# Masked scores computed in two 64-key halves on two column groups of TensorE, with a new order from entry 480 on

## The chip, the cores and the metric

The kernel runs on one core of one Trainium2 chip. The metric is device time of one execution in microseconds (us). Each core has TensorE (PE, with its weight loads shown apart as PEld), VectorE (DVE), ScalarE (ACT), GpSimd (POOL) and SyncE (SP, which here issues most of the DMAs). Measured differences under about 0.5% count as none.

## The reference, cut to what matters

Two layers follow each other. The first is a linear recurrence over the sequence with a complex decay, for 4 batches, 8 heads, 768 positions and 48 dimensions; the second is a feed-forward layer with the activation h * tanh(softplus(h)).

```python
mag = np.sqrt(a_re * a_re + a_im * a_im)
scale = np.minimum(mag, 0.999) / (mag + 1e-06)
for t in range(S):
    S_re, S_im = (ar * S_re - ai * S_im + kv, ar * S_im + ai * S_re)   # kv = k[t] outer v[t]
    y[:, :, t] = np.einsum('bhd,bhde->bhe', q[:, :, t], S_re)
h = x @ w_in                      # x: 3072 tokens x 384, w_in: 384 x 2048
sp = np.where(h > 20.0, h, np.log1p(np.exp(np.minimum(h, 20.0))))
out = (h * np.tanh(sp)) @ w_out   # w_out: 2048 x 384
```

## The kernel before, in words

The work is cut into 12 units of 256 positions, three for each batch. A unit is two chunks of 128 positions, called u3a and u3b for unit 3.

For each unit, ACT and DVE first turn the decay into running magnitudes and phases and multiply q and k by their growth, sine and cosine (lines 449 to 546). DMAs on SP relay the result into a tile `T` per chunk, with 96 rows (48 cosine, 48 sine) and for each of the 8 heads 128 columns of q and 128 of k.

The attention of a chunk then runs on TensorE, in groups of four heads (g = 0 and 1):

- `kn` (line 609) transposes k into PSUM, and a copy brings it to SBUF.
- `am` (line 623) computes the scores, 128 keys by 128 queries for each head, into a PSUM tile `pa`: one matmul a head in the source. In the trace every fp32 matmul is two loads and two matmuls, so a group of four heads is eight matmuls.
- `am_out` (line 630, DVE) multiplies `pa` by the causal mask into the SBUF tile `am`. A query sees keys up to its own position, so a quarter of each score matrix (keys 64 to 127, queries 0 to 63) is all zero.
- `y` (line 641) adds `am` times V and the old state `S` times q in `ypsum`. Even heads write PSUM partitions 0 to 47 and odd heads 64 to 111, so a pair of heads uses the two column halves of the array.
- `pd` (line 656) computes the new state. Each head is two matmuls, of 64 and of 33 output rows, again on the two column halves. `S add` (lines 665, 667) follows on DVE.

The feed-forward part takes each unit's y as x. For each of 8 pairs of columns, `mm1` (line 751) fills a PSUM tile `ph`, then come exp, cap, square, ln and inv on ACT and DVE, `gate`, `gh` and `gl`, and `mm2` (line 788) adds into `po`. Here the matmul runs on fp32r, with each operand split in two halves (xH, xL, wh, wl, gh, gl).

Nothing schedules this at run time. All operations are recorded in a list and issued in the order of the table `ORDER` (lines 54 to 152), whose letters can pick the engine. Each engine then works its own queue strictly in that order and waits on semaphores. So PE's order decides which matmuls stand next to each other, and how much other PE work lies between a score group and the `ypsum` matmuls that read its mask product.

Of the kernel before, what the change touches and what calls it, by code (L numbers as in the profile page):

```python
# [45 lines left out]
HELD = 2  # L46
XRUNS = ((0, 0, 0, 32), (0, 1, 32, 16), (64, 1, 64, 16), (0, 2, 80, 32))
# [18 lines left out]
306 397 744 400 307 246V 398 446 299 401 257 248 579 322 396 399 308 402 249 403 448 405 580 313 748 404 250 406 323  # L66
# [3 lines left out]
342 602 598 338 331 425 344 604 427 268 269 601 339 463 749 747 345 609 270 346 462 607 751 261V 605 475 347 933 271V  # L70
444 599 340 752 348 608 606 754 474 756 932 349 757 341 437 458 419 350 464 456V 476 439 351 416 465 759 466 610 441
352 612 487 353 613 611V 354 443 750 614 355 600 477 467 753G 445 486 745 468 746 478 616 758 479 615 469 621 617 488
618 755 470 622 447 619 623 449 480 626 489 624 471 499 760 490 498 940 481 491 451 511 500 625 492 510 764 620 501
628 493 502 482A 494 522 761 503 512 472 454 513 523 763 453 504 627 473 937 505 630 762 629 455 524 631 514 483 535
515 525 765 526 766 534 516 495 767A 517 484 527 768 632 485 528 774 636 506 536 459 496 633 771 769 634 518 507 497
772 635 537 529 508 519 530A 509 773 775A 770 546 639 641 640 460 777 547 637 538 520 548 531 521 784 539 532 938 549
787 642 533 540 638 785 941G 550 541 778 643 551 457 786 939 644 779 542A 790 655 552 543 780 645 942 783 544 788 461
944 545 789 553 782 945 656 943 781 554 1123 668 555 953 646 791 657 954 793 946 556 955 792 794V 647 956 557 648 658
667 957 558 649 559 795 560 1124 650 659 561 1128V 797 947 796 669 679 798 651A 948 660 802 670 776 949 671 800 935
661 799 934 803 1129 804 958 936 806 1131 662 680 950 1130 691 681 672 807V 692 673 805 682 952 674 808 810 809 652  # L80
951 801V 812 683 811 653 693 813 663A 1133 684 814 965A 963 675A 815 685 961 817 816V 964A 960 819 664 654 959 686 823
694 825 665 962 967 824 1135 822 703 695 676 968 704 974 973 716 971 705 696 706 666 975 1144 1132 697 978 828 677 698
707 977 1136 966 1145 1305 715 970 830 687 976 728 717 972 708 718 727 688 969 709 1134 980 826 678 719 979 699 720
831 1304 689 710 721 1146 829 1137 690 700 729 818 1125 827 701 1138 1147 1126 711A 702 722 1139 832 820 1148 821 833
712 730 981 1312V 834 713 1140 723A 982 845 724 731 1141 983 985 984 732 714 733 1142 734 725 1309 1149 844 1143 735
835 856 736 836 1155G 986 1150 726 1154 1151V 1153 737 1152 987 1157 846 857 738 988 837 1158 838 992 739 994 741 993
740 839 1127 997 989 742 995 858 1156 847 1310 998V 990 996 848 1313G 999 991V 1163 1001 1000 840 1162 849 1003 1161
1311 841 1160 869 850 1002 1494 1314 842 851 1316 868 1004 1317 1325 1005 859 1006 1315 860 1008 1326 1164 861 1010
862 880 852A 1007V 1167 870 881 1493 871 1169 1011 872 863 843 1165 873 853 1013 882 892 874 1166 883 1318 875 1014
854 884 1327 1170 1319 893 1159 1320 864A 1016 1328 855 894 865 1015 885 1321 1168 905 886 895 1017 904 1009 896 1018  # L90
887 897 866 876 1307 906 1019V 877 898 1306 867 1501 1020 899 1498 878 907 888 908 1021V 1171 1022 1499 1173 900 917
1322 909 1172 916 910 1174V 879 918 919 1024 1329 920 1500 1502 1175 1324 1177 1176 1506 889 1023 921 911 1323 890
1012 922 1504 1335G 912A 891 1178 1025 1336G 1036 1026 1503 1180 1332V 1334 1179 1182 1330 901 1184 913 1035 923 1183
924A 902 1185 1331 1186G 903 914 925 1333 1685 1338 915 1027 1505 926 1028 1345 1339 927 1341 1514 1047 1037 1346 928V
1507 1038 1343 1515 1048 1039 1348 1029 1181V 1351 1187 1040 929 930 1030 1189 1308 1508 1340 1509 1060 1516 1049 1188
1344 1041 1190 931 1191 1342 1050 1337 1517 1192 1042 1059 1193 1031 1518 1051 1194 1032 1071 1052 1347 1510 1043A
1350 1033 1053 1349 1061 1072 1196 1062 1054 1063 1684 1034 1197 1064 1195 1073 1352 1065 1495 1354 1074 1083 1044
1055A 1496 1075 1056 1045 1689 1066 1692V 1076 1084 1202V 1511 1077 1096 1200 1690 1095 1198V 1085 1078 1067A 1199
1046 1201 1097 1519 1108 1079A 1086 1098 1087 1203 1057 1512 1068 1099 1058 1100 1069 1353 1080 1101 1513 1070 1088
1526G 1107 1355 1089 1356 1691 1090 1524 1358 1091A 1521 1081 1102 1204 1357 1109 1092 1205 1103 1082 1110 1359 1111  # L100
1217 1104 1206 1112 1363 1113 1360 1364 1207 1361 1694 1365 1693 1696 1367 1093 1368 1114 1362 1520 1115 1216 1525A
1366 1528 1094 1218 1208 1105 1116 1529 1209 1522V 1106 1219 1523 1117 1228 1697 1535 1118 1865 1369 1371 1533 1370
1220 1534 1373 1210 1372 1531 1119 1229 1121 1211 1122 1374 1241 1120 1230 1705 1497 1221 1231 1537 1240 1695 1232
1536 1233 1706 1375 1532 1234 1538 1376 1222 1530 1698 1223 1378 1866 1212A 1235 1539 1380 1699 1377V 1253 1242 1381
1386 1243 1540 1252 1213 1244 1383 1224A 1264 1541 1245 1225 1384 1246 1700 1214 1254 1701 1870 1265 1379 1236 1527
1255 1686 1215 1247 1256 1385 1871 1226 1237 1687 1266 1276 1257 1267 1707 1391V 1872 1248 1542 1702 1258 1544 1277
1392 1227 1708 1238 1259 1387V 1278 1389V 1239 1249 1268 1279 1269 1388 1288 1390 1270 1250 1873 1271 1704 1875 1874G
1289 1280 1382 1393 1281 1260A 1394 1545 1290 1261 1703 1251 1291 1272A 1876 1262 1282 1292 1716 1283 1263 1715A 1293
1273 1543 1284 1406 1878 1709 1710 1879 1546 1712V 1294 1548 1395 1295 1711 1274 1547 1881 1275 1549 1285 1877 1405
1714 1713 1553 1407 1555 1296 1286 1297 1718 1287 1298 1554 1556 1408 1396 1299 1409 1886 1397 1418 1398 1300V 1725  # L110
1399 1417 1410 1880 1558 1302V 1550 1727 1400 1719 1559V 1551 1401A 1688 1557 1419 1887 1560 1882 1730 1562 1561 1723
1552 1564 1722 1411 1563 1301 1430 1565 1720 1717 1303 1883 1566 1721 1726 1567 2055 1569 2054 1568V 1420 1571 1402
1421 1429 1575 1412 1422 1572 1731 1403 1431 1724 1423 1432 1576 1404 1433 1424 1729 1434 1413 1441 1577 1425A 1728
# [95 lines left out]
def tile_kernel(ctx, tc, q, k, v, are, aim, are_t, aim_t, w_in, w_out, out):  # L209
# [866 lines left out]
```

## Time and profile before

| | |
|---|---|
| three runs | 586.17, 586.56, 588.39 us (median 586.56) |
| profiled execution, first to last instruction | 585.6 us |
| PE busy / PEld busy | 574.0 us (98%) / 540.2 us (92%) |
| DVE busy / ACT busy / POOL busy | 470.4 us (80%) / 474.2 us (81%) / 24.1 us (4%) |
| mean granted TensorE clock | 0.997 |
| DMA | 67.10 MB, mean 115 GB/s |

The profiled execution is listed by its span alone. The runs' median lies 1.0 us above that span. A matmul's duration in the trace holds its way through the array, so neighbours overlap: the rate of a stream is read from the distance between starts, not from the duration of one.

### The profile page before, as it was taken

What the parts mean: (1) busy time and instruction counts of PE and PEld (TensorE: products, weight loads), DVE (VectorE), ACT (ScalarE), POOL (GpSimd) and SP (SyncE); (2) the same over time, 40 slices, a digit from 0 to 9 for tenths busy, and PEclk for the clock granted to TensorE, in tenths of its full rate; (3) what the DMA queues carried; (4) which work ended last, traced back from release to release, by engine and by line L of the source; (5) the groups of instructions that cost most, each with busy time, mean ns of one, the idle gap of its engine ahead of it and who ended that gap; (6) DMA issues with size and microseconds to landing.
All of it is one profiled execution on the core that took longest, in us unless ns stands there. A gap on an engine that the chain in (4) does not pass through costs nothing.

```text
span 585.6 us, 12607 instructions
## 1 busy us (share of the span) xinstructions
PE 574.0 (98%) x4974; PEld 540.2 (92%) x4974; DVE 470.4 (80%) x830; ACT 474.2 (81%) x762; POOL 24.1 (4%) x57
## 2 busy tenths in 40 slices
PE   8999999999999999999999999999999999999996
PEld 4679887899999999999999999999999999999995
DVE  6999999999999889886779978778777865465453
ACT  7899999899997999689988869876974966555572
POOL 2010000101000100000001001001000000000000
PEclk9999999999999999999999999999999999999998
DMA  8788865403637252280081082272064042001000
GB/s 288 256 258 268 282 223 152 140 4 93 176 85 188 73 152 77 65 235 2 26 215 59 2 241 58 55 216 56 10 177 113 1 125 84 32 8 28 29 1 31
DMA packets 57170, 67.10 MB, mean 115 GB/s; under 512 B 4832, under 2 KB 50144, under 8 KB 57104
## 3 DMA queue, kind: packets, MB, share of 16 engines
q1 hardware_dynamic: 56320, 65.37, 37.8%
q8 instruction: 41, 0.67, 0.5%
q10 hardware_dynamic: 720, 0.66, 0.4%
q14 instruction: 25, 0.20, 0.1%
q0 software_dynamic: 64, 0.20, 0.1%
HBM read 37.75 MB, written 4.72 MB: 73 GB/s over the span
## 4 chain that ended last, share of the span: by engine, by line
PE 61%; ACT 18%; DVE 12%; issue 4%; DMA 2%; SPq 1%; POOL 0%; DVEq 0%; ACTq 0%; POOLq 0%
PE ph L751 25%; PE po L788 23%; ACT e L173 6%; ACT X L173 5%; PE ypsum L641 4%; PE pa L623 4%; ACT L171 4%; PE pd L656 2%; PE pkn L609 2%; DVE g L764 1%; DVE am L630 1%; DVE gl L776 1%; DVE X L546 1%; ACT I L173 1%; DVE e L820 1%
## 5 line engine op out<-in xcount | busy, mean ns | idle before, releaser
L173 ACT ACTIVATE e<-e 128x512 f32<-128x512 f32 x192 | 118.2, 627 | 32.7 <-DVE e L820 31.4
L751 PE MATMUL ph<-xH,wh 128*128 128x256 f32 x462 | 133.3, 288 | 0.8 <-DVE g L764 0.7
L751 PE MATMUL ph<-xH,wl 128*128 128x256 f32 x462 | 129.8, 281 | 0.0
L751 PE MATMUL ph<-xL,wh 128*128 128x256 f32 x462 | 129.7, 281 | 0.0
L788 PE MATMUL po<-wh,gh 128*128 128x384 f32 x308 | 105.1, 341 | 0.0
L788 PE MATMUL po<-wh,gl 128*128 128x384 f32 x308 | 103.8, 337 | 0.0
L788 PE MATMUL po<-wl,gh 128*128 128x384 f32 x308 | 103.5, 336 | 0.0
L751 PEld LDWEIGHTS ph<-xH,wh 128*128 128x128 f32 x462 | 87.0, 188 | 3.3 <-DVE g L764 1.7
L751 PEld LDWEIGHTS ph<-xL,wh 128*128 128x128 f32 x462 | 87.0, 188 | 0.3
L751 PEld LDWEIGHTS ph<-xH,wl 128*128 128x128 f32 x462 | 87.0, 188 | 0.0
L764 DVE SCALAR_TENSOR_TENSOR g<-e,ph 128x512 f32<-128x512 f32 x96 | 65.3, 681 | 27.0 <-ACT e L173 25.2
L173 ACT ACTIVATE e<-ph 128x512 f32<-128x512 f32 x96 | 56.5, 590 | 33.3 <-PE ph L751 28.9
L776 DVE TENSOR_TENSOR gl<-g,gh 128x512 fp32r<-128x512 f32 x88 | 60.0, 684 | 15.1 <-ACT gh L770 9.4
L173 ACT ACTIVATE e<-e,fifth 128x512 f32<-128x512 f32 x96 | 68.8, 719 | 1.3
L820 DVE TENSOR_SCALAR e<-e 128x512 f32<-128x512 f32 x96 | 40.2, 421 | 25.3 <-ACT e L173 25.0
L788 PEld LDWEIGHTS po<-wh,gl 128*128 128x128 f32 x308 | 57.9, 188 | 0.7 <-DVE gl L776 0.5
L788 PEld LDWEIGHTS po<-wh,gh 128*128 128x128 f32 x308 | 58.0, 188 | 0.3 <-issue 0.2
L788 PEld LDWEIGHTS po<-wl,gh 128*128 128x128 f32 x308 | 57.9, 188 | 0.0
L171 ACT ACT_TABLE_LOAD x44 | 56.5, 1283 | 0.7
L623 PE MATMUL pa<-T 96*128 96x128 f32 x384 | 49.4, 277 | 0.8 <-DVE am L630 0.8
L623 PEld LDWEIGHTS pa<-T 96*128 96x128 f32 x384 | 46.1, 191 | 2.0 <-DVE am L630 1.0
L770 ACT CAST gh<-g 128x512 fp32r<-128x512 f32 x43 | 26.3, 611 | 12.2 <-DVE g L764 11.8
(137 smaller groups left out, 1049.3 us busy)
## 6 DMA issues: line engine op xcount, KB each, us to landing
T<-QK SPq DMA_DIRECT2D x70, 129.0 KB, 3.1
T<-X SPq DMA_DIRECT2D x69, 129.0 KB, 3.2
words<-w_in SPq DMA_DIRECT2D x8, 768.0 KB, 5.8
words<-w_out SPq DMA_DIRECT2D x8, 768.0 KB, 5.0
QK<-k SPq DMA_DIRECT2D x12, 384.0 KB, 4.4
QK<-q SPq DMA_DIRECT2D x12, 384.0 KB, 4.3
V<-v SPq DMA_DIRECT2D x12, 384.0 KB, 4.4
R<-a_re SPq DMA_DIRECT2D x12, 384.0 KB, 4.0
```

Source lines behind the costliest of these rows:

```text
L171: self.nc.scalar.preload_act_table_set(need)
L173: return self.nc.scalar.activation(out, in_, func, **kw)
L609: e.transpose(d["pkn", g][:, i, :], T()[:, 4 * g + i, 1, :C], ident)
L623: e.matmul(d["pa", g][:, i, :], T()[:, 4 * g + i, 1, :C], T()[:, 4 * g + i, 0, :C], start=True, stop=True)
L641: e.matmul(ypsum[64 * par:64 * par + D, i, :], lhs, rhs, start=m == 0, stop=first or m == 1)
L656: e.matmul(d["pd", g][r, i, :], d["kn"][:, h, r], st["V"][:, c, h * D:(h + 1) * D], start=not held, stop=not held or i == 3)
L751: e.matmul(ph[k][:, slot(k, j, a), :], win(x, j, kt, a), st[y][:, kt, cols(k)], start=n == 0, stop=n + 1 == len(todo))
L764: e.scalar_tensor_tensor(g_[k], e_[k], 2.5, ph[k], ALU.subtract, ALU.mult)
L770: (e.copy if e is nc.scalar else e.tensor_copy)(gs[k][0], g_[k])
L776: e.tensor_tensor(gs[k][1], g_[k], gs[k][0].bitcast(F32), ALU.subtract)
L788: e.matmul(po[t], x[:, slot(k, j, a), 0 if halved else t * P:C if halved else (t + 1) * P], wout(y, j, a), start=j == 0 and a == 0 and n == 0,
L820: op("V", f"{n} cap", lambda e, k=k: e.tensor_scalar_min(e_[k], e_[k], math.exp(20.0)))
```

## The change

From unit 3 on (`HALF = 3`) a group of four heads is computed by halves of 64 keys. The first half (keys 0 to 63) meets all 128 queries, the second (keys 64 to 127) only queries 64 to 127; the quarter that the mask makes zero isn't computed. The even head of a pair writes keys 0 to 63 to PSUM partitions 0 to 63, the odd head to partitions 64 to 127, and for the second half the other way round, so that at any time one head of the pair is on either column half. In the odd heads the key rows are thus swapped, and a second copy of V for the odd heads with its rows rolled by 64 (`vs`, prepared outside the kernel and loaded by a DMA for each unit) takes V's place in `y`.

The mask product is written by three DVE instructions in place of one, into two tiles that are kept for the whole kernel and were set to zero once. The mask constant has a second copy for the swapped rows. `ORDER` keeps its first 480 entries; the rest is another order. One line of the table's difference stands for all.

```diff
+HALF = 3
-306 397 744 400 307 246V 398 446 299 401 257 248 579 322 396 399 308 402 249 403 448 405 580 313 748 404 250 406 323
+306 397 744 400 307 246V 398 446 299 401 257 248 579 322 396 399 308 402 249 403 448 405 580 313 749 404 250 406 323
...
-    cmask = const.tile([P, P], BF16, name="cmask")
-    nc.gpsimd.memset(cmask, 1.0)
-    nc.gpsimd.affine_select(
-        out=cmask, in_=cmask, compare_op=ALU.is_ge, fill=0.0, base=0,
-        pattern=[[1, P]], channel_multiplier=-1,
-    )
+    cmasks = const.tile([P, 2, P], BF16, name="cmask")
+    cmask = cmasks[:, 0]
+    nc.gpsimd.memset(cmasks, 1.0)
+    for r0, par, base in ((0, 0, 0), (0, 1, -64), (64, 1, 0)):
...
+    swapped = Tiles({"Vs": (wts, "w14", 1, [P, 2, NCH, DM // 2])})
+    masked = Tiles({g: (at, "am", 2, [P, 4, C]) for g in range(2)})
...
+        if u >= HALF:
+            st.homes["Vs"] = lambda: swapped["Vs"][:, u % 2]
+            op("S", f"Vs{u} load", lambda e: e.dma_start(st["Vs"], vs[u]))
...
-                    for i in range(4):
-                        e.matmul(d["pa", g][:, i, :], T()[:, 4 * g + i, 1, :C], T()[:, 4 * g + i, 0, :C],
-                                 start=True, stop=True)
+                    if u < HALF:
+                        for i in range(4):
+                            e.matmul(d["pa", g][:, i, :], T()[:, 4 * g + i, 1, :C], T()[:, 4 * g + i, 0, :C],
+                                     start=True, stop=True)
+                        return
+                    for i0 in (0, 2):
+                        for k0 in (0, C // 2):
+                            for i in (i0, i0 + 1):
+                                r0 = (k0 + C // 2 * (i % 2)) % C
+                                e.matmul(d["pa", g][r0:r0 + C // 2, i, k0:], T()[:, 4 * g + i, 1, k0:k0 + C // 2],
+                                         T()[:, 4 * g + i, 0, k0:C], start=True, stop=True)
...
+                    d["am", g] = masked[g]
+                    x, y = (t.rearrange("p (i two) t -> p i two t", two=2) for t in (d["am", g], d["pa", g]))
+                    m = cmasks.unsqueeze(1).broadcast_to([P, 2, 2, C])
+                    for r, two, t in ((slice(0, P), slice(0, 2), slice(C // 2, C)),
+                                      (slice(0, P // 2), 0, slice(0, C // 2)), (slice(P // 2, P), 1, slice(0, C // 2))):
+                        e.tensor_tensor(x[r, :, two, t], y[r, :, two, t], m[r, :, two, t], ALU.mult)
...
-                                lhs = st["V"][:, c, h * D:(h + 1) * D] if new else old["S"][:, h, :]
+                                if u >= HALF and par:
+                                    lhs = st["Vs"][:, c, i * D:(i + 1) * D]
+                                else:
+                                    lhs = st["V"][:, c, h * D:(h + 1) * D]
+                                lhs = lhs if new else old["S"][:, h, :]
...
+        if u == HALF:
+            for g in range(2):
+                op("GV", f"masked{g} zero", lambda e, g=g: e.memset(masked[g], 0.0))
```

PE's queue at the scores of u3a, in the kernel before: `pa` is the score tile, `ph` and `po` belong to the feed-forward part.

```order
L751 MATMUL ph<-xH,wl 128x256
L623 MATMUL pa<-T 128x128 x8
L751 MATMUL ph<-xH,wh 128x256
L751 MATMUL ph<-xL,wh 128x256
L751 MATMUL ph<-xH,wl 128x256
```

The same scores of u3a in the changed kernel (64x128 is a first half, 64x64 a second):

```order
L824 MATMUL po<-whl,gh 128x384
L644 MATMUL pa<-T 64x128 x2
L644 MATMUL pa<-T 64x64 x2
L644 MATMUL pa<-T 64x128 x2
L644 MATMUL pa<-T 64x64 x2
L644 MATMUL pa<-T 64x128 x2
L644 MATMUL pa<-T 64x64 x2
L644 MATMUL pa<-T 64x128 x2
L644 MATMUL pa<-T 64x64 x2
L824 MATMUL po<-whl,gh 128x384
```

Eight source matmuls become sixteen narrower ones, still between matmuls that use the full array. The scores of u7b in the kernel before stand between a transpose and `ph`, with no matmul of the column halves beside them:

```order
L641 MATMUL ypsum<-am,V 48x128 x2
L609 MATMUL pkn<-identity,T 128x96 x4
L623 MATMUL pa<-T 128x128 x8
L751 MATMUL ph<-xH,wh 128x256
L751 MATMUL ph<-xL,wh 128x256
```

In the changed kernel u7b's scores (one group of four heads here, the other group behind the last of these rows) stand between `ypsum` matmuls of u7a (`kept` is the kept mask product, `Vs` the rolled copy of V):

```order
L674 MATMUL ypsum<-kept,V 48x128
L674 MATMUL ypsum<-kept,Vs 48x128
L644 MATMUL pa<-T 64x128 x2
L644 MATMUL pa<-T 64x64 x2
L644 MATMUL pa<-T 64x128 x2
L644 MATMUL pa<-T 64x64 x2
L674 MATMUL ypsum<-T,S 48x128 x2
L674 MATMUL ypsum<-kept,V 48x128
L674 MATMUL ypsum<-kept,Vs 48x128
```

Here the scores moved next to work that also uses the column halves. Over the whole of PE's queue, blocks of matmuls on the column halves, each entered from and left to full-array matmuls, are 32 before and 40 now.

DVE's queue at the mask product of u3a, before, both groups (`e` and `g` are the feed-forward part's):

```order
L453 SCALAR_TENSOR_TENSOR X,good<-R 128x6x128
L630 TENSOR_TENSOR am<-pa,cmask 128x512 x2
L479 TENSOR_SCALAR X<-X 128x6x128
L820 TENSOR_SCALAR e<-e 128x512
```

And now:

```order
L521 TENSOR_SCALAR I<-X_1416 128x768
L659 TENSOR_TENSOR kept<-pa,cmask 128x4x64
L659 TENSOR_TENSOR kept<-pa,cmask 64x2x64 x2
L659 TENSOR_TENSOR kept<-pa,cmask 128x4x64
L659 TENSOR_TENSOR kept<-pa,cmask 64x2x64 x2
L856 TENSOR_SCALAR e<-e 128x512
```

One instruction of 512 elements a row became three, of 256, 128 and 128.

## Rows read from the trace of the kernel before

**Rows 1.** page, totals (busy us, share, xinstructions) and slices (tenths)
```profile
span 585.6 us, 12607 instructions
...
PE 574.0 (98%) x4974; PEld 540.2 (92%) x4974; DVE 470.4 (80%) x830; ACT 474.2 (81%) x762; POOL 24.1 (4%) x57
...
PEclk9999999999999999999999999999999999999998
```

**Rows 2.** page, chain that ended last, by engine, by line
```profile
PE 61%; ACT 18%; DVE 12%; issue 4%; DMA 2%; SPq 1%; POOL 0%; DVEq 0%; ACTq 0%; POOLq 0%
PE ph L751 25%; PE po L788 23%; ACT e L173 6%; ACT X L173 5%; PE ypsum L641 4%; PE pa L623 4%; ACT L171 4%; PE pd L656 2%; PE pkn L609 2%; DVE g L764 1%; DVE am L630 1%; DVE gl L776 1%; DVE X L546 1%; ACT I L173 1%; DVE e L820 1%
```

**Rows 3.** groups by form, PE and PEld: busy us, mean ns | idle
```profile
L623 PE MATMUL pa<-T 96*128 96x128 f32 x384 | 49.4, 277 | 0.8 <-DVE am L630 0.8
L623 PEld LDWEIGHTS pa<-T 96*128 96x128 f32 x384 | 46.1, 191 | 2.0 <-DVE am L630 1.0 <-DVE R L430 0.5 <-ACT kn L616 0.2
...
L656 PEld LDWEIGHTS pd<-V,kn 128*64 128x64 f32 x320 | 21.5, 137 | 3.2 <-issue 2.4 <-DVE am L630 0.2
...
L656 PEld LDWEIGHTS pd<-V,kn 128*33 128x33 f32 x320 | 18.1, 110 | 0.0
```

**Rows 4.** timeline of PE, one score group; first columns start and duration, us
```profile
401.16 0.34 PE L788 MATMUL po<-wl,gh 128*128 128x384 f32 x1
401.33 1.05 PE L623 MATMUL pa<-T 96*128 96x128 f32 x8
402.14 0.42 PE L788 MATMUL po<-wh,gh 128*128 128x384 f32 x1
```

**Rows 5.** timeline of PE, a block of ypsum between two ph
```profile
385.70 0.28 PE L751 MATMUL ph<-xL,wh 128*128 128x256 f32 x1
385.82 0.28 PE L751 MATMUL ph<-xH,wl 128*128 128x256 f32 x1
386.03 0.43 PE L641 MATMUL ypsum<-T,S 96*48 96x128 f32 x4
386.29 0.39 PE L641 MATMUL ypsum<-am,V 128*48 128x128 f32 x4
386.51 0.39 PE L641 MATMUL ypsum<-T,S 96*48 96x128 f32 x4
...
387.93 0.38 PE L751 MATMUL ph<-xH,wh 128*128 128x256 f32 x1
```

**Rows 6.** timeline of PE, a block of pd between po and pkn
```profile
199.22 0.34 PE L788 MATMUL po<-whl,gh 128*128 128x384 f32 x1
199.48 1.13 PE L656 MATMUL pd<-V,kn 128*64 128x48 f32 x32
200.61 0.55 PE L609 MATMUL pkn<-identity,T 96*128 96x96 f32 x4
```

**Rows 7.** groups by line and form, DVE
```profile
L630 DVE TENSOR_TENSOR am<-pa,cmask 128x512 f32<-128x512 f32 x48 | 32.4, 683 | 4.1 <-PE pa L623 4.0
...
L667 DVE TENSOR_TENSOR S<-pd,S 96x192 f32<-96x192 f32 x26 | 8.9, 349 | 4.3 <-PE pd L656 4.0
```

**Rows 8.** windows: stretch, length, busy us of PE, PEld, DVE, ACT, POOL
```profile
100.00:200.00 100.00, 99.17 (x862) 94.52 (x861) 95.56 (x158) 93.82 (x150) 4.72 (x6) 1.00 0.39 107
200.00:300.00 100.00, 99.06 (x943) 96.52 (x940) 82.31 (x144) 88.59 (x140) 3.89 (x9) 1.00 0.39 109
...
sum 480.00, PE 477.46 PEld 465.19 DVE 376.54 ACT 380.29 POOL 18.50; mean PE 95.49 PEld 93.04 DVE 75.31 ACT 76.06 POOL 3.70
```

**Rows 9.** waits of PE: us in total, times, longest
```profile
PE pd L673 <- DVE am L630: 1.3, 1, 1.3
PE pa L623 <- DVE am L630: 0.8, 1, 0.8
```

**Rows 10.** timeline, the end of the span
```profile
579.57 0.34 PE L788 MATMUL po<-whl,gh 128*128 128x384 f32 x1
580.08 0.49 ACT L799 ACTIVATE o<-po 128x384 f32<-128x384 f32 x1 [6.36 <-PE po L788]
```

More of the change, by code (lines that the diff above doesn't have):

```diff
@@ L74 @@
[L74 to L88, printed above, removed]
@@ new lines @@
+1393V 1394 1398 1244 1255 1552V 1256 1712 1295 1296 1265 1720V 1555 1266 1556 1550 1553 1554 1267 1278 1887 1888 1890
+1283 1284 1297 1503 1562 1560 1561 1298 1268 1279 1280 1399 1889 1299 1300 1301 1302 1723A 1884 1563 1564 1285 1286
+1287 1288 1400 1886 1895 1289 1694 1693 1722 1290 1567 1724 1719 1401 1402 1568V 1896 1565 1721 1726 1733 1412 1729
+1403 1404 1405 1406 1411 1407 1735 1413 1424 1414 1291 1725 1423 1425 1426 1292 1303 1304 1566V 1557 1569 1570 1305
+1306 1897 1558 1571 1572 1408 1307 1308 1898 1576 1415 1577 1696 1416 1417 1418 1419 1420 1737 1734 1731 1728 1559
@@ new lines @@
+1573 1427 1428 1429 1430 1574 1578 1579 1580 1736 1575 1727 1581 1584 2063 1435 1431A 1436 1437 1409 1585 1438 1583
+1439 1738 1440 1441 1460 1891 1892 1695 1442 1459 1740 1461 1448 1742 1739 2064 1582 1462 1586 1463 1876 1894 1410
+1589 1447 1464 1472 1465 1449 1450 1471 1587 1432 1421 1422 1451 1732 1452 1588 1433 1590 1875 1466 1443 1434 1444
+1741 1453 1473 1483 1743 1484 1474 1445 1454 1455A 1456 1446 1899 1744 1746 1457 1475 1485 1486 1467 1468 1745 1730
+1458 2072V 1469 1470 2069 1476 1477 1591 1478 1479 1480 2070 1900 1604 1481 1487 1488 1489 2071 2074G 1482 1490 1893
@@ L198, in __missing__ @@
     def __missing__(self, key):
-        pool, tag, bufs, shape, *dtype = self.homes[key]
-        name = key if isinstance(key, str) else key[0]
+        home = self.homes[key]
+        if callable(home):
+            self[key] = home()
+            return self[key]
+        pool, tag, bufs, shape, *dtype = home
+        name = key if isinstance(key, str) else "kept" if isinstance(key, int) else key[0]
         self[key] = pool.tile(shape, dtype[0] if dtype else F32, tag=tag, name=name, bufs=bufs)
@@ L208, in tile_kernel @@
 @with_exitstack
-def tile_kernel(ctx, tc, q, k, v, are, aim, are_t, aim_t, w_in, w_out, out):
+def tile_kernel(ctx, tc, q, k, v, vs, are, aim, are_t, aim_t, w_in, w_out, out):
     nc = tc.nc
@@ L223, in tile_kernel @@
     op.table = EXPLN
-    cmask = const.tile([P, P], BF16, name="cmask")
-    nc.gpsimd.memset(cmask, 1.0)
-    nc.gpsimd.affine_select(
-        out=cmask, in_=cmask, compare_op=ALU.is_ge, fill=0.0, base=0,
-        pattern=[[1, P]], channel_multiplier=-1,
-    )
+    cmasks = const.tile([P, 2, P], BF16, name="cmask")
+    cmask = cmasks[:, 0]
+    nc.gpsimd.memset(cmasks, 1.0)
+    for r0, par, base in ((0, 0, 0), (0, 1, -64), (64, 1, 0)):
+        x = cmasks[r0:, par] if par == 0 else cmasks[r0:r0 + 64, par]
+        nc.gpsimd.affine_select(
+            out=x, in_=x, compare_op=ALU.is_ge, fill=0.0, base=base,
+            pattern=[[1, P]], channel_multiplier=-1,
+        )
     halfpi = const.tile([P, 1], F32, name="halfpi")
```

145 lines of the change are left out of this document (76 added, 69 removed), and 3 rows, old and new, of the table ORDER.

## The prediction

> **What bounds the kernel now.** I read the totals first. PE is busy 574.0 of 585.6 us, DVE and ACT 80% and 81%, and the granted clock stands at its upper level (2.4 GHz) in every slice but the last [rows 1]. The chain that ended last confirms it: PE holds 61% of it, and the scores (`pa`) are 4% of the span there [rows 2]. So the kernel ends when PE's queue ends, and PE hardly waits: from 100 to 580 us it is without work for 480 - 477.5 = 2.5 us [rows 8], and over the whole span the named waits are one of 1.3 us and one of 0.8 us [rows 9], with trifles beside them. A change pays here if it shortens PE's queue itself, or costs if it makes PE wait. Then I read the distances between starts in the timeline, since durations overlap.
>
> **Price of a score group before.** Eight `pa` matmuls take 1.05 us from the first start to the last end [rows 4]. The last lasts 0.28 us [rows 3], so seven distances are 0.77 us: 0.111 us for one. A group of four heads holds PE for 8 x 0.111 = 0.89 us.
>
> **Price of a group now.** It is 16 matmuls in the trace (two for each of eight in the source): eight of 128 columns, eight of 64, and they alternate between the column halves of the array. No row shows scores in this form, but two rows show its parts. `ypsum` also streams 128 columns on both halves: four matmuls start every 0.22 us (386.29 to 386.51), so two side by side cost 0.11 us, as much as one full-width matmul does [rows 5]. `pd` loads 64 columns of weights for a stream of 48 on one half while the other half works on 33: 32 matmuls last 1.13 us [rows 6], minus the last one's way of about 0.22 us leaves 0.91 us for 16 pairs, 0.057 us a pair. A load of 64 columns costs about (191 - 137) / 64 x 64 = 54 ns, from the two widths' durations [rows 3], so `pd` is bound by its wide load. A second half of scores has that load and a stream of 64 columns, half of 0.111 us: also about 0.055. I take 0.11 and 0.057. For two heads that is 2 x 0.11 + 2 x 0.057 = 0.334 us, for a group 0.67 us. The gain is 0.22 us a group. Units 3 to 11 have 9 x 2 x 2 = 36 groups: **-7.9 us** on PE, all of it on the path.
>
> **Price of entering and leaving the column halves.** From the last `ph` before a block of `ypsum` (385.82) to the first `ph` after it (387.93) are 2.11 us. One `ph` is worth 0.12 (385.70 to 385.82) and 32 `ypsum` matmuls are worth 8 x 0.22 = 1.76. The rest, 0.23 us, is the array emptying on the way in and out [rows 5]. The `pd` block shows the same: `pkn` starts only at 200.61, exactly when `pd` ends [rows 6]. Scores did not pay this before: `pa` started 0.17 us after the last `po`, as the next `po` would have [rows 4]. Now they do, unless they stand beside `ypsum` or `pd`. PE's order has 40 such blocks now against 32, so 8 x 0.23 = **+1.8 us**. The Trainium skill has this as a rule: "TensorEngine Tiling (Array Packing)", section "Key Properties", says that changing the tiling mode drains TensorE. It speaks against the change, and the trace agrees with 0.23 us: had each of the 36 groups stood alone, the drain (36 x 0.23 = 8.3 us) would eat the whole gain.
>
> **DVE.** The mask product becomes three instructions of 256, 128 and 128 elements a row. From 683 ns for 512 and 349 ns for 192, an element costs 1.04 ns and an instruction 149 ns [rows 7]. Two more instructions are +0.30 us a group, 10.8 us in all. I cost them at nothing on the path: DVE has 100 - 82 = 18 us free from 200 to 300 us, and more later; only from 100 to 200 us is it nearly full, at 95.6 [rows 8], and there it takes units 3 and early 4, some 6 groups, 1.8 us against 4.4 us free. But the mask product also stands between the scores and `ypsum`, so the chain from the last score to its use grows from 0.68 to 0.98 us. Behind a late mask product PE's whole queue waits. What covers it is the PE work that the order puts between: a closer group has one `ypsum` and one `pd` group there (8 x 0.11 = 0.88 and 8 x 0.057 = 0.46, so 1.3 us), and most have several `ph` or `po` groups more. Without cover it is 0.30 us a group.
>
> **Edits at nothing.** Nine loads of rolled V (196 KB each) go through SP's queue in front of relays of `T`; PE has no named wait of any size for a DMA [rows 9], and the load for unit 3 stands behind the relays of u3a that PE needs first, with the two score groups, a `po` and a `ph` group (over 3 us) before its use. The two zeroings and the wider mask constant are POOL's, which is busy 4% [rows 1]; the spinning matmuls at the start wait only for the first of the three mask instructions. At the end, the verdict on the input range moves to the last twelve `po` matmuls. They last 12 x 0.17 = 2.1 us, and `o` starts 0.2 us after PE ends [rows 10], so a flag read within 2 us is hidden; I take 0, at most +0.5.
>
> **The other order.** No row prices it. Below, it can win back no more than PE's 2.5 us without work. Above, I take the worst hundred microseconds (0.94 us without work, 200 to 300 [rows 8]) for all 480, 4.5 us, which is 2.0 more than now. I take 0, since before and after the order leaves PE's queue equally dense by what I can read.
>
> **Sum.** On the profiled span: 585.6 - 7.9 + 1.8 = 579.5 us. The runs' median is 1.0 us above the span, so 586.56 - 6.1 = **580.5 us**. Its own range goes from 577.5 (2.5 us of waits gone, and a little more) to 583.0 (2.0 us of waits more, 0.5 at the end).
>
> **Rivals.**
>
> *The halves don't run beside each other (slower).* In `ypsum` and `pd` the halves strictly alternate in the queue; the new scores go first, second, second, first. If a matmul could only pair with its neighbour in the queue, each head pair would be three steps of 0.11 and three of 0.057, 0.50 us against 0.444: +0.056 x 72 pairs = +4.0, with the drains +5.8: 592.4 us. With no overlap at all it is 4 x 0.11 + 4 x 0.057 = 0.67, +16 us, 604. It decides from a head pair above 0.42 us (0.444 less the drains' 1.8 / 72). Against it: in `ypsum` the two trace matmuls of one head and the two of the next also share the queue two by two, and still two cost 0.11 [rows 5].
>
> The Trainium skill gives this rival a form of its own. "TensorE: Matmul & The Clock Gate", Part 3, "The mechanism", says that a load overlaps running matmuls only when their row groups differ, and all these matmuls use the same rows. As a mechanism here: each half waits with its load until its own matmul is through, 0.11 + 0.054 and 0.057 + 0.054 us, twice each, 0.55 us a head pair, +7.6 + 1.8: 596 us. The trace speaks against that: `pd` would need 0.054 + 0.04 us for a pair of matmuls and takes 0.057 [rows 6].
>
> *The mask product comes late.* If DVE's extra 0.30 us is uncovered in about 20 of the 36 groups, the gain of 6.1 us is gone (586.5); uncovered in 7 to 18 it leaves 582.6 to 585.9, in all 36 it gives 591. For it: DVE at 95.6% from 100 to 200 us [rows 8], and one wait of PE on that very product already [rows 9]. Against it: after 200 us DVE has room.
>
> *The new order wins more.* PE's waits vanish and fewer changes between `ph` and `po` help: 576 to 577.5. PE has little left to win.
>
> **How the numbers follow.** The forecast has 0.68. The late mask product has 0.19, of which 0.05 lie below 583.6, 0.10 within 0.5% (583.6 to 589.5, about what a measurement can tell from no change) and 0.04 above. The halves that don't overlap have 0.02 as neighbours that can't pair and 0.03 as loads that wait, all above 589.5. The better order has 0.05. The rest, 0.03, is a wait I don't see, within 0.5%. Faster: 0.68 + 0.05 + 0.05 = 0.78; same: 0.10 + 0.03 = 0.13; slower: 0.04 + 0.05 = 0.09. The range for 8 in 10 goes from 577.0 to 586.5: it holds the forecast's own range and the mask product late in up to 20 groups.
>
> **What would show it.** `pa` in units 3 to 11 should start a group's 16 matmuls within 0.67 us, and pairs of starts a few ns apart; 0.9 us or more falsifies the main term. The first full-array matmul behind a score block should start about when the block ends. PE should wait for the mask product no longer in total than about 2 us. DVE's busy time should rise by some 11 us and PE's span fall by 6. A `ypsum` that waits for a DMA, or a last `o` that starts more than 0.3 us after PE's end, would each make the cost "nothing" wrong.

## The result and the profile after

The changed kernel took 580.25 us (median of 4 runs, 579.42 to 580.87), the kernel before 587.47 us beside it (4 runs, 586.17 to 589.87): a ratio of 0.9893, 95% interval 0.9862 to 0.9924. A second set of runs gave 580.09 against 587.68 us, 0.9874 (0.9845 to 0.9903). The forecast was 580.5 us. The profiled execution has a span of 579.2 us against 585.6.

The page's totals, answering to [rows 1], and the engines' shares of the chain that ended last, answering to [rows 2]:

```profile
span 579.2 us, 13318 instructions
...
PE 566.4 (98%) x5262; PEld 532.2 (92%) x5262; DVE 486.1 (84%) x899; ACT 476.2 (82%) x763; POOL 27.4 (5%) x59
...
PEclk9999999999999999999999999999999999999998
...
PE 77%; ACT 10%; DVE 9%; issue 2%; POOL 1%; ACTq 0%; DVEq 0%; POOLq 0%
```

PE has 288 matmuls more and is busy 7.6 us less. It still sets the end, now with 77% of the chain, and the granted clock is as before. DVE is busy 15.7 us more; the mask product's share of that is worked out below.

The groups by form of the scores and of the mask product (busy us, mean ns | idle), answering to [rows 3] and [rows 7]:

```profile
L644 PEld LDWEIGHTS pa<-T 96*64 96x64 f32 x576 | 27.0, 136 | 3.0 <-issue 0.7 <-DVE S L700 0.6 <-DVE X L515 0.2
L644 PE MATMUL pa<-T 96*64 96x128 f32 x288 | 26.8, 280 | 0.2 <-DVE S L700 0.2
...
L644 PE MATMUL pa<-T 96*64 96x64 f32 x288 | 21.2, 220 | 0.0
L659 DVE TENSOR_TENSOR kept<-pa,cmask 64x128 f32<-64x128 f32 x72 | 20.4, 283 | 0.7
...
L659 DVE TENSOR_TENSOR kept<-pa,cmask 128x256 f32<-128x256 f32 x36 | 15.1, 421 | 10.9 <-PE pa L644 6.3 <-PE ypsum L674 4.2
```

By its means the mask product of a group is 421 + 2 x 283 = 987 ns, against 683 ns [rows 7]: the +0.30 us of the prediction. But neighbours on DVE overlap, as they do on PE. From the start of the first of the three instructions to the end of the last a group takes 0.92 us (median of 36), so the chain from the scores to their use grew by 0.24 us. One group (start and duration, us):

```profile
206.86 0.91 DVE L659 TENSOR_TENSOR kept<-pa,cmask 128x256 f32<-128x256 f32 x3
```

Of the 15.7 us more on DVE, 6.7 are there too when the new order keeps the single mask instruction (e2 below, busy 477.1 us). The three instructions bring the other 9.0, 0.25 us a group.

PE's timeline (start and duration, us) in three places: two score groups together between `po`, one group between `ph` and `ypsum`, one group alone. They answer to [rows 4]:

```profile
312.44 0.34 PE L824 MATMUL po<-wl,gh 128*128 128x384 f32 x1
312.71 1.56 PE L644 MATMUL pa<-T 96*64 96x128 f32 x32
314.20 0.44 PE L824 MATMUL po<-wh,gh 128*128 128x384 f32 x1
314.48 0.34 PE L824 MATMUL po<-wh,gl 128*128 128x384 f32 x1
...
443.88 0.28 PE L787 MATMUL ph<-xH,whl 128*128 128x256 f32 x1
444.09 0.89 PE L644 MATMUL pa<-T 96*64 96x128 f32 x16
444.81 0.39 PE L674 MATMUL ypsum<-T,S 96*48 96x128 f32 x4
...
487.69 0.28 PE L787 MATMUL ph<-xH,whl 128*128 128x256 f32 x1
487.90 0.89 PE L644 MATMUL pa<-T 96*64 96x128 f32 x16
488.72 0.44 PE L824 MATMUL po<-wh,gh 128*128 128x384 f32 x1
```

Four pairs of heads hold PE from 312.71 to 314.20, 1.49 us with the way out. Inside the block the starts repeat every 0.335 us (313.096 to 313.431), and the two starts of a pair lie 7 to 10 ns apart. The reader should also look one matmul further: the first `po` behind the block holds PE for 0.28 us (314.20 to 314.48) in place of its usual 0.17. Behind the `ypsum` block of the kernel before [rows 5] it is the same: the `ph` at 387.93 holds PE for 0.22 us in place of 0.12, as the next start shows:

```profile
388.15 0.28 PE L751 MATMUL ph<-xL,wh 128*128 128x256 f32 x1
```

DVE by stretches, answering to [rows 8], and PE's waits, answering to [rows 9] (us, times, longest):

```profile
100.00:200.00 100.00, 99.57 (x933) 94.95 (x933) 98.17 (x169) 97.11 (x158) 5.67 (x9) 1.00 0.42 118
200.00:300.00 100.00, 99.74 (x1027) 96.67 (x1024) 92.66 (x178) 88.63 (x139) 7.55 (x9) 1.00 0.41 116
```

```profile
PE po L824 <- DVE gl L812: 0.4, 1, 0.4
...
PE pd L689 <- DVE kept L659: 0.3, 1, 0.3
PE pa L644 <- DVE S L700: 0.2, 1, 0.2
```

DVE is at 98% and 93% in the two stretches where it was at 96% and 82%, yet PE's one named wait for the new mask product is 0.3 us.

The end of the span, answering to [rows 10]:

```profile
571.10 0.34 PE L824 MATMUL po<-whl,gh 128*128 128x384 f32 x1
571.52 0.49 ACT L835 ACTIVATE o<-po 128x384 f32<-128x384 f32 x1 [6.01 <-PE po L824]
574.33 0.35 SPq L841 DMA_DIRECT2D out_dram<-o  x1
```

and the same store in the kernel before, whose `o` ended at 580.57:

```profile
580.59 0.34 SPq L805 DMA_DIRECT2D out_dram<-o  x1
```

The last store leaves 2.32 us behind the end of `o` (572.01) in place of 0.02 us. Counted from PE's last start that is 3.23 against 1.02 us, 2.2 us later. The repetition of the changed kernel (the second set above) has the store as late:

```profile
570.93 0.49 ACT L835 ACTIVATE o<-po 128x384 f32<-128x384 f32 x1 [6.01 <-PE po L824]
573.69 0.35 SPq L841 DMA_DIRECT2D out_dram<-o  x1
```

But its span ends 3.05 us behind the store's issue, against 4.86 us here and 5.04 in the kernel before. In all the traces this last stretch is either 3.0 to 3.1 or 4.5 to 5.0 us, with a late store and with a prompt one; what sets it, no run shows. So the 2.2 us of the store are the change's, while the rest of the tail differed by 1.8 us between two executions of the same kernel.

**Where the time went.** The two programs are alike up to the 790th matmul of PE. From there to PE's last start the kernel before needs 480.18 us, the changed one 471.30: -8.88. The start of the span took 0.41 us longer in this execution, and from PE's last start to the span's end it is 8.09 against 6.06 us, +2.03. The sum is -6.4 us. (In the repetition PE's path is 471.39 us and the tail 6.24.)

### The profile page after: what moved, and what is told of

Its sections match the earlier page's. It is cut to its first block, busy times and chain, and to the rows that moved or that the text cites. A ratio compares the mean times of both kernels' runs of the same rounds, so it can differ in the third digit from the quotient of the medians.

```text
span 579.2 us, 13318 instructions
## 1 busy us (share of the span) xinstructions
PE 566.4 (98%) x5262; PEld 532.2 (92%) x5262; DVE 486.1 (84%) x899; ACT 476.2 (82%) x763; POOL 27.4 (5%) x59
## 4 chain that ended last, share of the span: by engine, by line
PE 77%; ACT 10%; DVE 9%; issue 2%; POOL 1%; ACTq 0%; DVEq 0%; POOLq 0%
PE po L824 32%; PE ph L787 32%; PE ypsum L674 5%; PE pa L644 4%; ACT X L174 4%; PE pd L689 2%; ACT e L174 2%; PE pkn L622 2%; ACT L172 2%; DVE X L559 1%; DVE w L296 1%; DVE QK L535 1%; DVE g L800 1%; DVE wl L323 1%; ACT words L174 1%
## 5 line engine op out<-in xcount | busy, mean ns | idle before, releaser
L174 ACT ACTIVATE e<-e 128x512 f32<-128x512 f32 x192 | 119.6, 629 | 29.9 <-DVE e L856 27.8
L856 DVE TENSOR_SCALAR e<-e 128x512 f32<-128x512 f32 x96 | 44.1, 462 | 15.2 <-ACT e L174 14.8
L659 DVE TENSOR_TENSOR kept<-pa,cmask 64x128 f32<-64x128 f32 (+1 forms) x108 | 32.6, 329 | 11.5 <-PE pa L644 6.3
L674 PE MATMUL ypsum<-T,S 96*48 96x128 f32 x320 | 33.9, 276 | 0.0
L806 ACT CAST gh<-g 128x512 fp32r<-128x512 f32 x38 | 23.4, 617 | 12.2 <-DVE g L800 12.1
```

The source lines that it names most:

```text
L174: return self.nc.scalar.activation(out, in_, func, **kw)
L659: e.tensor_tensor(x[r, :, two, t], y[r, :, two, t], m[r, :, two, t], ALU.mult)
L674: e.matmul(ypsum[64 * par:64 * par + D, i, :], lhs, rhs, start=m == 0, stop=first or m == 1)
L806: (e.copy if e is nc.scalar else e.tensor_copy)(gs[k][0], g_[k])
L856: op("V", f"{n} cap", lambda e, k=k: e.tensor_scalar_min(e_[k], e_[k], math.exp(20.0)))
```

## Experiments

Each was timed in five rounds beside the kernel before. "PE's path" is the distance named above, from the shared start to PE's last matmul. "Late starts" are the sum over starts on that path that come more than 0.2 us later than the usual distance behind their predecessor (0.12 us behind a `ph` or a whole score, 0.17 behind a `po`, 0.08 behind a `pkn`, 0.055 behind a `ypsum` or a half score, 0.03 behind a `pd`). This shows waits better than idle time does, which begins only when the last matmul's duration in the trace is over.

| kernel | time, us | ratio to before (95%) | PE's path, us | late starts, us | blocks on the halves |
|---|---|---|---|---|---|
| before | 586.6 to 587.7 | 1 | 480.18 | 4.1 | 23 |
| changed kernel | 580.25 | 0.9893 (0.9862 to 0.9924) | 471.30 | 1.6 | 31 |
| changed kernel, second set | 580.09 | 0.9874 (0.9845 to 0.9903) | 471.39 | 1.5 | 31 |
| e2, new order, whole scores | 585.91 | 0.9987 (0.9972 to 1.0002) | 476.25 | 0.4 | 26 |
| e5, e2 with three mask instructions | 585.27 | 0.9953 (0.9936 to 0.997) | 476.23 | 0.4 | 26 |
| e10, before with three mask instructions | 588.30 | 1.0006 (0.9988 to 1.0024) | 481.75 | 5.5 | 23 |
| e3b, halves in the old order | 593.25 | 1.0094 (1.0064 to 1.0124) | 485.35 | 10.1 | 45 |
| e4, pairs alternate | 581.05 | 0.9902 (0.9882 to 0.9923) | 471.29 | 1.4 | 31 |
| e6, wide streams on one half | 586.30 | 0.9985 (0.9967 to 1.0003) | 477.22 | 0.4 | 31 |
| e7, quarter masks twice | 595.98 | 1.0135 (1.0106 to 1.0164) | 486.53 | 15.5 | 31 |
| e1, verdict 20 us earlier | 580.93 | 0.991 (0.989 to 0.9931) | 473.66 | 4.1 | 31 |
| e1b, verdict a little earlier | 579.78 | 0.985 (0.9823 to 0.9878) | 473.45 | 3.3 | 31 |
| e1c, verdict read in a gap of DVE | 578.88 | 0.9843 (0.9826 to 0.986) | 472.22 | 2.3 | 31 |

(The blocks are those behind the shared start; the kernel has 9 more ahead of it, the same in all.)

**e2: the new order without the halves.**

```diff
+FULL = UNITS
...
-                    if u < HALF:
+                    if u < FULL:
                         for i in range(4):
...
-                    for r, two, t in ((slice(0, P), slice(0, 2), slice(C // 2, C)),
-                                      (slice(0, P // 2), 0, slice(0, C // 2)), (slice(P // 2, P), 1, slice(0, C // 2))):
-                        e.tensor_tensor(x[r, :, two, t], y[r, :, two, t], m[r, :, two, t], ALU.mult)
+                    e.tensor_tensor(d["am", g], d["pa", g], cmask.unsqueeze(1).broadcast_to([P, 4, C]), ALU.mult)
...
-                                if u >= HALF and par:
+                                if u >= FULL and par:
```

> The changed kernel with its new order, but scores again as one 128-key matmul a head, one mask instruction, and plain V for the odd heads; the rolled V is still loaded. Theory (the halves are the gain): 36 groups cost 0.22 us more each (+7.9), and blocks on the column halves fall from 40 to 35 (-1.15 at 0.23): +6.8, to about 587.0, as slow as the kernel before. Rival (the new order is the gain): the time stays within 2 us of 580.2.

Measured: 585.91 us. The theory's 587.0 was nearer than the rival's time, but not for its reason: on PE's path the order alone is worth -3.93 us and the halves, within this order, the other -4.95. What hides the order's part is that e2's last store, too, leaves 2.7 us late:

```profile
576.91 0.49 ACT L832 ACTIVATE o<-po 128x384 f32<-128x384 f32 x1 [6.01 <-PE po L821]
580.10 0.35 SPq L838 DMA_DIRECT2D out_dram<-o  x1
```

So the order gives back 2.6 of its own 3.9 us at the end (the store leaves 3.61 us behind PE's last start, 576.49, in place of 1.02), and e2 as a whole is not faster than before by more than the measurement tells.

**e5: DVE's part of the change added to e2.**

```diff
-                    e.tensor_tensor(d["am", g], d["pa", g], cmask.unsqueeze(1).broadcast_to([P, 4, C]), ALU.mult)
+                    for r, two, t in ((slice(0, P), slice(0, 2), slice(C // 2, C)),
+                                      (slice(0, P // 2), 0, slice(0, C // 2)), (slice(0, P // 2), 1, slice(0, C // 2))):
+                        e.tensor_tensor(x[r, :, two, t], y[r, :, two, t], m[r, :, two, t], ALU.mult)
```

> New order, scores of 128 keys by 128 queries with one matmul a head and plain V as in e2, but the mask product in three DVE instructions (256, 128 and 128 elements a row): only DVE's part of the change is added to e2 (585.9 us). Theory A, the new order covers the longer mask product (it was made with it): 585.9 to 587, ratio to before 0.998 to 1.001, PE's waits below 1.5 us. Rival B, it is exposed as in e7 (there 0.44 us of PE's path for each 0.57 us of DVE's): 36 x 0.31 x 0.76 = 8.5 us more, 594, ratio 1.013, with PE waiting for the mask product and for g.

Measured: 585.27 us and a PE path of 476.23 against 476.25. Theory A stands for what e5 adds, but e5 adds less than the change does. DVE is busy 479.9 us, 2.8 more than in e2 where the change adds 9.0, and a group takes 0.81 us in place of 0.92:

```profile
206.08 0.80 DVE L660 TENSOR_TENSOR kept<-pa,cmask 128x256 f32<-128x256 f32 x3
```

In e5 both quarters lie on partitions 0 to 63, and the third instruction starts 0.197 us behind the second. In the changed kernel the third lies on partitions 64 to 127 and starts 0.286 us behind (medians), with no wait between them in the trace. So e5 shows that 0.13 us more a group cost PE nothing in this order. For the whole +0.24 the bound is the step from e2 to the changed kernel, where late starts grow by 1.2 us and 0.2 us stays unattributed. (That e5's time is even 0.6 us lower than e2's has nothing on PE's path behind it: the two were timed in different sets, and the shared start took 98.95 us in e5's trace and 100.12 in e2's.)

**e10: the same in the old order.** The edit is that of e5, for units 3 to 11 of the kernel before, with the two quarters written on all 128 partitions.

> The kernel before with its own order and its own scores; only the mask product of units 3 to 11 is written in three DVE instructions (256, 128 and 128 elements a row). It parts what e3b lost against its expectation (593.25 instead of 583.8) into DVE's share and the share of the column halves' blocks. Theory A, DVE's longer mask product is exposed in the old order: about 0.3 us in most of the 36 groups, 594 to 597, ratio 1.013 to 1.018. Rival B, the old order covers it and e3b's loss lies in the drains and in V's loads: 586.6 to 588, ratio 1.000 to 1.003.

Measured: 588.30 us, a ratio of 1.0006. PE's path is 1.6 us longer, 1.4 of it in late starts. The durations of the mask instructions add up to 11 us more, but they overlap: DVE is busy only 3.2 us more (473.6 against 470.4), and a group takes 0.815 us from first start to last end, 0.13 more than before. This much the old order nearly covers, and B was the closer one. e10 doesn't hold the other half of what the change adds. The two forms of the mask product there:

```profile
L636 DVE TENSOR_TENSOR am<-pa,cmask 128x128 f32<-128x128 f32 x72 | 17.3, 282 | 0.0
L636 DVE TENSOR_TENSOR am<-pa,cmask 128x256 f32<-128x256 f32 x36 | 15.1, 420 | 3.7 <-PE pa L623 3.6
```

**e7: the quarter masks twice.**

```diff
                         e.tensor_tensor(x[r, :, two, t], y[r, :, two, t], m[r, :, two, t], ALU.mult)
+                        if r != slice(0, P):
+                            e.tensor_tensor(x[r, :, two, t], y[r, :, two, t], m[r, :, two, t], ALU.mult)
```

> The changed kernel with the two narrow mask instructions of each group issued twice (same values): two more instructions of 128 elements, about 0.5 us a group on DVE and in front of the group's use, 18 us in all. Theory (the mask product is covered by PE's work): DVE's busy time rises by 15 to 20 us and the time by under 1 us. Rival (the mask product is late in many groups): the time rises by 0.5 us for each group without cover, up to 18 us.

Measured: 595.98 us, 15.7 us more than the changed kernel, for 20.2 us more on DVE (506.3 against 486.1); a group's mask product takes 1.57 us in place of 0.92. PE's waits, and PE and DVE (third and fifth number) from 200 to 300 us:

```profile
PE pd L691 <- DVE kept L661: 4.0, 6, 1.4
PE ph L789 <- DVE g L802: 1.9, 4, 0.6
...
PE ypsum L676 <- DVE kept L661: 0.8, 4, 0.2
```

```profile
200.00:300.00 100.00, 96.82 (x976) 92.73 (x975) 93.91 (x183) 83.94 (x133) 8.32 (x9) 1.00 0.38 106
```

So the theory of this run, under 1 us, is refuted, and its rival holds. The change's own 9.0 us on DVE cost PE's path at most about 1.4 us (e2 to the changed kernel, as above), the next 20.2 cost 15.2. The cover that the prediction counted on exists, but the change has used it up.

**e3 and e3b: the halves in the old order.** The table's part behind entry 480 is the old one; the loads of rolled V stand behind those of V, the two zeroings ahead of u3a's scores.

```diff
-457 787 943 644 780 542A 791 655 552 543 781 645 946 784 544 789 461 948 545 790 553 783 949 656 947 782 748 554
+457 787 943 644 780 542A 791 655 552 543 781 645 946 784 544 789 461 748 948 545 790 553 783 949 656 947 782 554
```

(A line of e3b's table against e3's: 748 is a load of rolled V.)

> The halves in the order of the kernel before: the scores by halves, three mask instructions, rolled V (each load behind the unit's last relay in SP's queue), every other entry where it was. Blocks on the column halves are 54 in this order, against 32 before and 40 in the changed kernel. Theory (drain of 0.23 us a block): -7.9 + 22 x 0.23 = -2.8 against the kernel before, about 584; the new order's own part is then the rest, some 3.5 us, of which 14 x 0.23 = 3.2 are blocks. Rival (drains are cheap, the halves carry it alone): about 579. Rival (mask product late, 0.3 us a group): 590 or more.

e3's loads stood ahead of the last use of the tile that they overwrite, so that odd heads worked with another unit's V; it took 597.56 us (ratio 1.0185), which is not the time of the halves in the old order. e3b has them behind it.

> The halves in the order of the kernel before, with each load of rolled V right behind the unit's load of V (in e3 it stood before the last use of the unit two before, so e3 computed with a wrong V and waited there). 54 blocks on the column halves against 32 before and 40 in the changed kernel. Theory (0.23 us a block): -7.9 + 22 x 0.23 = -2.8, about 583.8. Rival (drains cheap): 579. Rival (the mask product uncovered in the old order, 0.3 us a group): 590 or more.

Measured: 593.25 us, 9.5 us above the expectation. The rival's number, 590 or more, was met. Whether its reason was too, e10 doesn't settle: there the mask product is 0.13 us a group longer and DVE busy 3.2 us more, here 0.25 (0.93 us a group) and 11.8 (482.2 us). The trace shows two things. The first is one group alone between `po`, the very place of [rows 4]:

```profile
405.68 0.34 PE L815 MATMUL po<-wl,gh 128*128 128x384 f32 x1
405.94 0.89 PE L635 MATMUL pa<-T 96*64 96x128 f32 x16
406.76 0.45 PE L815 MATMUL po<-wh,gh 128*128 128x384 f32 x1
407.05 0.34 PE L815 MATMUL po<-wh,gl 128*128 128x384 f32 x1
```

Less a `po` on either side, 407.05 - 405.68 - 2 x 0.173 = 1.02 us. The whole-array group in its place cost 0.90 us, counted the same way (the second `po` behind it starts at 402.40). So a lone group loses 0.12 us. Two together, in the changed kernel, cost 314.48 - 312.44 - 2 x 0.173 = 1.69 us against 2 x 0.896: 0.05 gained a group. Only a group beside `ypsum` or `pd` gains the whole 0.22, or nearly: at 444.09 above `ypsum` starts 0.72 us behind it, and between two `ypsum` at 332.00 the next one starts 0.67 us behind. The old order has 10 groups alone, 24 in twos and 2 beside column work: +1.2 - 1.2 - 0.4, which is nothing. The changed kernel has 1, 16 and 19. The second is late starts: 10.1 us against 4.1, of which e10 explains 1.4. PE's named waits on this path end mostly with products of DVE and ACT, and one of 0.5 us with a DMA, a relay of `T` and not a load of rolled V:

```profile
PE ph L778 <- DVE g L791: 2.2, 3, 1.1
PE po L815 <- DVE gl L803: 1.1, 2, 0.6
PE pa L635 <- ACT kn L620: 0.9, 2, 0.8
...
PE pkn L613 <- DMA T<-QK: 0.5, 1, 0.5
```

What makes the other 4.6 us, DVE's longer mask product or PE that comes sooner to the same products, no run separates.

**e4 and e6: how the halves are fed.** In e4 the second halves go odd head first, so that the column halves strictly alternate. In e6 both heads' wide streams use one half of the array, both narrow ones the other.

```diff
-                            for i in (i0, i0 + 1):
+                            for i in (i0, i0 + 1) if k0 == 0 else (i0 + 1, i0):
```

> The changed kernel, but in the second halves the odd head's matmul goes first, so that the column halves alternate strictly in PE's queue (first, second, first, second) in place of first, second, second, first. Theory (each column half is fed from the queue past what waits for the other): a head pair stays at 0.335 us and the time within 0.5 us of 580.2. Rival (a matmul pairs only with its neighbour in the queue): a head pair gets shorter and the time falls by up to 4 us.

```diff
-                                r0 = (k0 + C // 2 * (i % 2)) % C
+                                r0 = k0
...
-                                if u >= HALF and par:
+                                if u >= UNITS and par:
```

> The changed kernel, but both heads of a pair write keys 0 to 63 to the first column half and keys 64 to 127 to the second (no swapped rows, plain V). So the queue goes first, first, second, second, and the two wide streams share one half. Theory (each half is fed past what waits for the other, but not without bound): the wide streams alone need 4 x 0.107 = 0.43 us a head pair, so at best +0.095 x 72 = +6.8, 587; with nothing overlapped 0.67 us, +24, 604. The place between tells how far ahead the queue feeds a half; the trace's distance from pair to pair settles it.

Two groups between `po`, first e4, then e6:

```profile
314.45 0.34 PE L824 MATMUL po<-wl,gh 128*128 128x384 f32 x1
314.72 1.56 PE L644 MATMUL pa<-T 96*64 96x128 f32 x32
316.21 0.44 PE L824 MATMUL po<-wh,gh 128*128 128x384 f32 x1
```

```profile
314.42 0.34 PE L824 MATMUL po<-wl,gh 128*128 128x384 f32 x1
314.68 1.96 PE L644 MATMUL pa<-T 96*64 96x128 f32 x32
316.57 0.44 PE L824 MATMUL po<-wh,gh 128*128 128x384 f32 x1
```

e4's block is the changed kernel's to the hundredth, 1.49 us, and so is PE's path; its time, 581.05 us, is not told apart from 580.25 (their intervals overlap). The theory of e4 holds. e6's is 1.89 us: 0.40 more for four pairs of heads, so a pair costs 0.335 + 0.10 = 0.435 us, four wide streams of 0.109. The narrow ones on the other half cost nothing beside them. In these three arrangements each half is fed by itself: what a block costs is the longer of two sums, one for each half, whatever the order within the pair. With 72 pairs that is +7.2 us, about the best case of e6's expectation; PE's path grew by 5.9, with 1.2 us of late starts gone (e6's mask product is as short as e5's, 0.81 us a group).

**e1, e1b and e1c: the verdict.** Eight entries of the table that lead to the verdict on the input range are moved forward; e1 and its two successors differ in the last two, the sum on PE and its reading on DVE.

```diff
+ORDER = moved(ORDER, ((2342, 2062), (2341, 2342), (2343, 2350), (2289, 2351), (2344, 2367), (2345, 2344), (2346, 2372), (2347, 2379)))
```

> The changed kernel with the input verdict (its last test, tally, sum and judge) moved some 25 us earlier in the order; all else as in the changed kernel. Theory (the late verdict is exposed): in the changed kernel SP branches on the flag 0.5 us before PE ends, and its next instruction comes 3.6 us after the branch, so the last store is issued 2.3 us after o is ready. With the branch far ahead the store follows o at once, the time from PE's last start to the end of the span falls from 8.1 to about 6.1 us, and the median falls by 2.0 us, to about 578.3. Rival (the end of the program simply varies, or the store waits for something else): the tail stays at 8 us and the time at 580.2.

e1: 580.93 us. The store leaves at once. The tail is even 3.92 us, since only 2.98 us follow the store in this execution. But PE waits 2.3 us for the sum that DVE hands it late:

```profile
PE ptotal L908 <- DVE total L904: 2.3, 1, 2.3
```

```profile
574.78 0.49 ACT L848 ACTIVATE o<-po 128x384 f32<-128x384 f32 x1 [6.29 <-PE po L837]
575.29 0.34 SPq L854 DMA_DIRECT2D out_dram<-o  x1
```

```diff
-(2346, 2372), (2347, 2379)
+(2346, 2383), (2347, 2393)
```

> As e1, but the sum on PE and the judge on DVE stand some 10 us before PE's end in place of 27 us, behind the test that they wait for. In e1 the store did follow o at once (issued 0.02 us after o's end, against 2.3 us in the changed kernel), but PE waited 2.3 us for the sum's input, and the prefix took 0.9 us longer. Theory (exposed branch, and e1 only moved the wait to PE): no wait of PE at the sum, the store at once, from PE's entry 790 to its last start 471.3 us as in the changed kernel; the median falls by about 2 us against the changed kernel, to 578.3. Rival (the store's end is set by something else than its issue): no gain.

e1b: 579.78 us, not 578.3; the store leaves at once, but now DVE itself waits 2.25 us for PE's sum, and PE later 1.8 us for `gl` and `g`.

```diff
-(2346, 2383), (2347, 2393)
+(2346, 2383), (2347, 2411)
```

> As e1b, but DVE's reading of the verdict's sum stands behind the exponential's cap of pair 5, where DVE waits 2.1 us for ACT, in place of a point where DVE itself waited 2.25 us for PE's sum. Theory: the last store leaves at once after o, as in e1b, and PE's waits for gl and g (1.8 us there) go back to about 0.5: the tail behind PE's last start is 4 to 6 us against 8.1 in the changed kernel, and the time is 577.5 to 579.5 on a chip where before takes 586.6, ratio 0.983 to 0.987. Rival: the store is late again since SP learns of the verdict too late, ratio 0.989 as the changed kernel.

> The changed kernel itself, beside e1c on the same chip, so that the two can be compared directly. It should give 580 to 581 on a chip where before takes 586.6 (ratio 0.989 as at first), with its last store again more than 2 us behind the last o. If e1c's ratio lies below this one's interval, the late verdict costs the changed kernel about 2 us.

e1c: 578.88 us, against 580.09 for the changed kernel on the same chip. Its end:

```profile
573.97 0.49 ACT L848 ACTIVATE o<-po 128x384 f32<-128x384 f32 x1 [6.29 <-PE po L837]
574.49 0.34 SPq L854 DMA_DIRECT2D out_dram<-o  x1
```

The store leaves 0.03 us behind `o`, where the changed kernel's own repetition was again late by 2.27 us. PE's path is 0.9 us longer than in the changed kernel, so about 1.4 us should remain, and the medians differ by 1.2. The two intervals overlap (0.9826 to 0.986 and 0.9845 to 0.9903), so the size is uncertain; e1c is the fastest version measured, though not clear of e1b (0.9823 to 0.9878).

## Why the prediction was right, and which of its steps were not

The time was right to 0.3 us (the gain, forecast at 6.1 us, is 6.4 by the spans and 7.2 and 7.6 by the medians of the two sets), and the main mechanism was. But two steps that were costed at nothing and one price were not. Their errors cancelled by luck: +0.9 us for the blocks, -2.5 for late starts, about -1 that stays unattributed, and +2.0 at the end.

| on PE's path, us | predicted | before to e2 | e2 to changed | both |
|---|---|---|---|---|
| score streams, 36 groups | -7.9 | 0 | -8.1 | -8.1 |
| blocks on the halves | +1.8 (8 x 0.23) | +1.0 (3 x 0.34) | +1.7 (5 x 0.34) | +2.7 |
| late starts | 0 | -3.7 | +1.2 | -2.5 |
| not attributed | | -1.2 | +0.2 | -1.0 |
| measured | | -3.93 | -4.95 | -8.88 |

- **Score streams: right.** The period of a pair of heads is 0.335 us, the prediction's sum 0.334; a whole-array group costs 0.896 us, the prediction had 0.89. The way in which `ypsum` and `pd` [rows 5, 6] gave the price of a form that no row showed held to a few ns. The rival that halves might not run beside each other is refuted by that period and by e4. The Trainium skill, "TensorE: Matmul & The Clock Gate", Part 3, "The mechanism", says that a load overlaps running matmuls "only when row_grp differs". The measured 0.335 us against the 0.55 worked out by that sentence says that for two column halves it does not hold.
- **The price of a block: too small.** The prediction read 0.23 us from the last `ph` before a block to the first `ph` after it [rows 5]. It did not look at how long that first `ph` holds PE. To the second matmul behind the block the excess is 0.31 to 0.35 us in `ypsum`, `pd` and score blocks alike where `ph` or `po` follows without a wait, and about 0.28 where `pkn` does. The row showed it: that `ph` lasts 0.38 us, its like 0.28. The Trainium skill's rule in "TensorEngine Tiling (Array Packing)", "Key Properties", that a change of tiling mode drains the array, agrees with all of these.
- **The order: not nothing.** "Above and below" was bounded by PE's 2.5 us without work. But starts on the path were late by 4.1 us in the kernel before, where PE is idle for only 2.4 us, since a matmul's duration in the trace counts as work to its end. The longest is 0.95 us at 291.80, behind a wait for DVE's mask product. e2 has 0.4 us of late starts. This is the step that failed most in size, and the rival of the better order had the mechanism right.
- **DVE at nothing: right to about 1 us, and at the edge.** From e2 to the changed kernel late starts grow by 1.2 us, and 0.3 us is the one named wait for the product. The sizes were a little high: the chain grew by 0.24 us a group and DVE's work by 9.0 us, in place of 0.30 and 10.8, because durations of neighbours overlap. e5 and e10 lengthen the product by half as much (0.0 and 1.6 us on PE's path), e7 shows how little cover was left. The rival of the late mask product was wrong for this change; whether it was right for e3b stays open.
- **The end: not nothing.** The prediction let the flag take up to 2 us, hidden by the last twelve `po`. From the end of DVE's write of the verdict (569.67) to the store's issue it takes 4.66 us. In the trace SP loads the flag at 569.70 and compares at 570.56, and its next instruction starts only at 574.17. The bound of +0.5 us for the end was passed: the store leaves 2.2 us later behind PE's last start. The sign that the prediction named, a last `o` more than 0.3 us behind PE's end, did not show it: `o` starts 0.09 us behind (571.43 to 571.52), and what was late is the store behind the branch.
- **Loads of rolled V and the zeroings: right.** PE has no named wait for either in the changed kernel.

## What to carry to other kernels

Work on column halves costs the longer of the two halves' sums plus some 0.34 us for every block that is entered and left, so ask for each group what stands beside it: the same edit gained 0.22 us beside other column work, 0.05 in twos, and lost 0.12 alone. Count an in-order queue's waits by late starts and not by idle time, take the length of several neighbours from the first start to the last end and not as a sum of durations, and price the order of a program apart from the edit in it. For a branch on a computed flag count up to the branching engine's next instruction, and give the verdict's sum places where neither engine stands waiting for the other.

## What the runs showed of the hardware

- In the changed kernel SP needed 3.6 us from its compare and branch (570.56) to its next instruction (574.17), and DVE 3.2 us (570.33 to 573.50); ACT and POOL took about 0.5 us for their branch on the same flag.
- A mask product of 128 elements a row lasts 283 ns on 64 partitions (changed kernel) and 282 ns on 128 (e10): by duration the number of partitions costs nothing. But on other partitions than the one ahead it starts later: 0.286 us behind it in the changed kernel (partitions 64 to 127 behind 0 to 63), 0.197 us in e5, e6 and e10, where both start at partition 0.
- A queue order of first, second, second, first half and a strict alternation take the same time to the hundredth of a us (e4).
